# K in one transfer per block, its last quarter copied aside on ScalarE, and wo read two heads at a time, in a cached decode attention kernel

## The chip, the cores and the metric

The kernel runs on one core of a Trainium2 chip. The metric is the device time of one execution in microseconds (us). The core has TensorE (PE: matmuls, and PEld, the weight loads), VectorE (DVE), ScalarE (ACT), GpSimd (POOL) and SyncE (SP), which here does nothing but issue transfers; 16 DMA engines move data between HBM and the on-chip memory SBUF.

## The reference, cut to what matters

One token of decode attention, mixed by a gate with a small token mixer. With D = 448, 16 query heads, 8 key/value heads (so two query heads share one), 65,536 cached keys and head size 256, all in bf16:

```python
g = sigmoid((x * gate_w).sum(-1, keepdims=True))
q = (x @ wq)                                   # 16 heads of 256
scores = einsum("bhqd,bhkd->bhqk", q, repeat(k_cache, 2)) * 256 ** -0.5
o = einsum("bhqk,bhkd->bhqd", softmax(scores), repeat(v_cache, 2))
a = o.reshape(1, 1, 4096) @ wo                 # 4096 x 448
b = gelu_mlp_over_tokens(layernorm(x))         # w1, b1, w2, b2
return g * a + (1 - g) * b
```

The K and V caches are 8 x 65,536 x 256 bf16 each, 268 MB each, and every byte is read once.

## The kernel before, in words

The caches are cut into 32 blocks of 16,384 keys (`NBLK`, four blocks per key/value head, `NB = 4`); block n has K(n) and V(n) of 8 MB each. `L` is the last block, 31. A block lies in SBUF as 128 partitions by 128 keys by 256 (64 KB in each partition). K lies in two tiles `kn0` and `kn1` of 64 keys per partition each (32 KB rows), V in one tile `vt`. There is one buffer for K and one for V: each is filled again when its readers are done, piece by piece, for the dependencies go by the bytes that are touched.

For each block, `score_block` (L370) goes through eight slices of 16 keys per partition. For each slice, `transposes` (L354) is one VectorE instruction that turns the slice into one of two buffers `kT`, and `scores` (L362) is eight matmuls into one PSUM tile. `softmax` (L416) then finds the maximum, takes the exponential on ScalarE (L441) and transposes the result into `pT` (L449). `products` (L510) multiplies with V in 64 matmuls (L384) and adds into an accumulator. At the end of every fourth block `head_end` (L497) normalises the result and multiplies it by two heads of `wo` (L493).

A helper `seq` keeps each engine's instructions in program order, so the order on the queues is the order of the Python code. In the main loop (L529 to L580), for block n up to 29, SyncE issues V(n) (L121; it waits until the products of block n-1 have read `vt`), then the two halves of K(n+1) (L115; the first waits for transposes 0 to 3 of block n, the second for 4 to 7). The transfers run in one queue behind each other. In block 0, `load_wo` (L129) then reads the first 14 heads of `wo` into the tile `wo_sb`, whose first part has served until then as the buffer `gel` of the mixer (written at L255, read at L321).

The end has an order of its own. In block 30 the queue gets the first 48 keys per partition of V(30) (3 MB), the two halves of K(31), and the rest of V(30) (5 MB). In block 31 V(31) is read in eight pieces into the buffers of K (L136), each as soon as the transposes of block 31 have left its place, and then the last two heads of `wo`. At the start, K(0) is read in three pieces, and `vt` holds the weights `wq` until the queries are made.

Of the kernel before, what the change touches and what calls it, by code (L numbers as in the profile page):

```python
# [8 lines left out]
FP32 = mybir.dt.float32  # L9
BF16 = mybir.dt.bfloat16  # L10
# [4 lines left out]
HQ = 16  # L15
HKV = 8
DH = 256
REP = HQ // HKV

BLK = 16384  # L20
VP = BLK // 128
KP = VP // 2
NJ = 16
NI = VP // NJ
NQ = 4
NW = DH // 2 // 32
QW = 128 + 2 * NI


@with_exitstack  # L30
def kernel(
# [15 lines left out]
    nc = tc.nc  # L47

    D = A_x.shape[-1]
# [3 lines left out]
    NF = F // 128  # L53
    NB = SK // BLK
    NBLK = HKV * NB
# [4 lines left out]
    def seq(ins):  # L60
        e = ins.ins.engine
        if e in last:
            tc.add_manual_dep(
                ins.ins,
                last[e],
                mybir.DependencyInfo(
                    mybir.DependencyClass.NoSync, mybir.DependencyReason.DATA
                ),
                reason="program order",
            )  # L70
        last[e] = ins.ins.name
        return ins

    kvpool = ctx.enter_context(tc.tile_pool(name="kvpool", bufs=1))
    const = ctx.enter_context(tc.tile_pool(name="const", bufs=1))
# [2 lines left out]


    kvpool.tile([128, 4096 - 128], mybir.dt.uint8, name="fill")  # L80
    k_tiles = [kvpool.tile([128, KP, DH], BF16, name=f"kn{i}") for i in range(2)]
    vt = kvpool.tile([128, VP, DH], BF16, name="vt")
    kT_tiles = [kvpool.tile([128, NJ, NW, 32, 2], BF16, name=f"kT{i}") for i in range(2)]
    p_sb = work.tile([128, 512], BF16)
    pT_tiles = [work.tile([128, 512], BF16, name=f"pT{i}") for i in range(2)]
    wo_sb = const.tile([128, HQ, 2, D], BF16)

    sc_tiles = [psum.tile([128, 512], FP32, name=f"sc{i}") for i in range(2)]
    pv_ps = psum.tile([128, 2, DH], FP32, name="pv_ps")
# [1 line left out]
    MC = D // 2  # L91
# [12 lines left out]
    DM = 384  # L104
    wq_m = vt[:, 0:48, :].rearrange("p a b -> p (a b)").rearrange("p (k n) -> p k n", k=3)
    wq_t = vt[:, 48:56, :].rearrange("p a b -> p (a b)")
    gel = wo_sb[:].rearrange("p h c n -> p (h c) n")[:, 0:NF, :]

    def rows(cache, n):
        g, b = divmod(n, NB)  # L110
        return cache[0, g, b * BLK:(b + 1) * BLK, :].rearrange("(p j) d -> p j d", j=VP)

    def load_k(n, h, pieces=((0, KP),)):
        for j0, j1 in pieces:
            seq(nc.sync.dma_start(  # L115
                out=k_tiles[h][:, j0:j1, :],
                in_=rows(A_k_cache, n)[:, h * KP + j0:h * KP + j1, :],
            ))

    def load_v(n, j0=0, j1=VP):  # L120
        seq(nc.sync.dma_start(out=vt[:, j0:j1, :], in_=rows(A_v_cache, n)[:, j0:j1, :]))  # L121

# [4 lines left out]

    def load_wo(h0, h1):
        seq(nc.sync.dma_start(  # L129
            out=wo_sb[:, h0:h1],  # L130
            in_=A_wo[h0 * DH:h1 * DH, :].rearrange("(h p c) n -> p h c n", p=128, c=2),
        ))

    def load_v_last(n):
# [9 lines left out]
        out=wq_t[:, :], in_=A_wq[DM:D, :].rearrange("r (h n) -> (r h) n", h=2)  # L144
    ))
    with nc.allow_non_contiguous_dma(reason="short rows"):
# [16 lines left out]
        out=val[:], in_=rowsel[:, :, :, 0:NI], op=ALU.add, axis=AXIS.XY  # L163
    ))
    fst = const.tile([128, 2, REP], FP32)
    for e in range(2):
        seq(nc.vector.tensor_reduce(
            out=fst[:, e, :], in_=rowsel[:, :, :, e:e + 1], op=ALU.add, axis=AXIS.XY
# [3 lines left out]
        out=par[:], in_=ident_f[:].rearrange("p (a r) -> p r a", r=REP), op=ALU.add, axis=AXIS.X  # L172
# [3 lines left out]
        out=nval[:], in0=val[:], scalar1=-scale, scalar2=None, op0=ALU.mult  # L176
# [7 lines left out]
        out=same[:], in_=val[:].unsqueeze(1).to_broadcast([128, 64, REP])  # L184
# [4 lines left out]
    for i in range(2):  # L189
# [3 lines left out]
        out=sel[:],  # L193
        in_=ident[:].rearrange("p (w k) -> p w k", w=NW).unsqueeze(2).to_broadcast([128, NW, NQ, 32]),
# [7 lines left out]
        out=xrr[:], in_=xr[:, DM:D].unsqueeze(2).to_broadcast([1, D - DM, 2])  # L202
    ))
    x_col = hd_ps[:, 40:44]
    for k in range(3):
        seq(nc.tensor.matmul(
            x_col[:, k:k + 1], lhsT=xr[:, 0:DM].rearrange("o (p k) -> o k p", k=3)[:, k, :],
            rhs=ones_b[:, 0:1], start=True, stop=True,
# [3 lines left out]
        rhs=ones_b[:, 0:1], start=True, stop=True,  # L212
# [6 lines left out]
        out=xtm[:], in0=par[:], scalar1=x_col[:, 3:4], scalar2=None, op0=ALU.mult  # L219
# [17 lines left out]
        out=veps[:], in0=mv[:, 1:2], scalar1=1e-5, scalar2=None, op0=ALU.add  # L237
# [5 lines left out]
    for _ in range(2):  # L243
# [3 lines left out]
            out=ntmp[:], in0=ntmp[:], scalar1=-0.5, scalar2=1.5, op0=ALU.mult, op1=ALU.add  # L247
# [3 lines left out]
        out=h_bc[:], in0=xf[:], scalar1=mv[:, 0:1], scalar2=rstd[:, 0:1],  # L251
        op0=ALU.subtract, op1=ALU.mult,
    ))
    for b in range(NF):
        seq(nc.scalar.activation(  # L255
            out=gel[:, b, :], in_=h_bc[:], func=ACT.Gelu_apprx_tanh,
# [4 lines left out]
    for h in range(HQ):  # L261
        half, hh = divmod(h, HQ // 2)
        for c in range(2):
            col = c * HQ + h
            for k in range(3):
                seq(nc.tensor.matmul(
                    q_ps[:, col:col + 1],
                    lhsT=wq_m[:, k, h * DH:(h + 1) * DH].rearrange("p (d c) -> p c d", c=2)[:, c, :],
                    rhs=xm[:, k:k + 1],
# [5 lines left out]
                lhsT=wq_t[:, hh * DH:(hh + 1) * DH].rearrange("p (d c) -> p c d", c=2)[:, c, :],  # L275
                rhs=xtm[:, half:half + 1],
# [6 lines left out]
    for w in range(NW):  # L283
        seq(nc.tensor.matmul(
            qq_ps[:, w * 2 * HQ:(w + 1) * 2 * HQ],
            lhsT=sel[:, w, :, :].rearrange("p a k -> p (a k)"), rhs=qb[:],
# [60 lines left out]
    oT = work.tile([128, 2, REP], BF16)  # L347
# [2 lines left out]
    res = const.tile([1, D], BF16)  # L350
    gcol = const.tile([128, 1], FP32)

    def transposes(i):
        seq(nc.vector.transpose(  # L354
            out=kT_tiles[i % 2][:].rearrange("p j w k c -> p (j w k c)").bitcast(FP32),
            in_=k_tiles[i // 4][:, i % 4 * NJ:(i % 4 + 1) * NJ, :].rearrange("p j d -> p (j d)").bitcast(FP32),
        ))

    def scores(n, i):
        for w in range(NW):  # L360
# [7 lines left out]
                ))  # L368

    def score_block(n, hooks={}):  # L370
        for i in range(NI):
            transposes(i)
            scores(n, i)
            if i in hooks:
                hooks[i]()
        if n % NB == 1 and n < NBLK - NB:
            place_q(n // NB + 1)
# [110 lines left out]
    def project(g):  # L488
        a_ps = hd_ps[0:1, 0:D]
        for r in range(REP):  # L490
            for c in range(2):
                seq(nc.tensor.matmul(  # L492
                    a_ps, lhsT=oT[:, c, r:r + 1], rhs=wo_sb[:, g * REP + r, c, :],  # L493
                    start=(r == 0 and c == 0), stop=(r == REP - 1 and c == 1),
                ))

    def head_end(g):  # L497
# [6 lines left out]
            seq(nc.vector.tensor_copy(out=a_acc[:], in_=a_ps))  # L504
        else:
            seq(nc.vector.tensor_tensor(out=a_acc[:], in0=a_acc[:], in1=a_ps, op=ALU.add))  # L506

    L = NBLK - 1

    def products(n):  # L510
        for ip in range(NI // 2):
# [17 lines left out]
    for n in range(NBLK):  # L529
        if n == 0:  # L530
            score_block(n, {2: gate_sum, 5: mixer_tail})
        elif n < L:
            score_block(n, {1: gate_column} if n == 1 else {})
        else:
            score_block(n, {1: result_base, 2: lambda: pv(L - 1, 0), 3: lambda: pv_one(L - 1, 2)})
        if n < L - 1:
            load_v(n)
            load_k(n + 1, 0)
            load_k(n + 1, 1)
            if n == 0:  # L540
                load_wo(0, HQ - REP)
        elif n == L - 1:
            load_v(n, 0, 48)
            load_k(L, 0)
            load_k(L, 1)
            load_v(n, 48, VP)
        else:
            load_v_last(L)
            for h in range(HQ - REP, HQ):
                load_wo(h, h + 1)  # L550
        if n < L:
            softmax(n)
        else:
            def rest_base():
                for k in range(2):
                    seq(nc.tensor.matmul(
                        f_rows[k], lhsT=ident_f[0:1, 0:1], rhs=base[0:1, k * MC:(k + 1) * MC],
                        start=True, stop=False, tile_position=(0, 32 * k),
                    ))
                pv(L - 1, 2, range(4, NJ))  # L560

            softmax(n, [lambda: pv_one(L - 1, 3), lambda: pv(L - 1, 2, range(4)), rest_base])
            seq(nc.vector.tensor_scalar(
                out=lsv[:], in0=val[:], scalar1=lsum[:, 0:1], scalar2=None, op0=ALU.mult
            ))
            pv(L - 1, 3)
            accumulate(L - 1)
            seq(nc.tensor.matmul(
                sm_ps[:, 456:456 + REP], lhsT=ones_f[:, :], rhs=lsv[:, :], start=True, stop=True
            ))  # L570
            seq(nc.vector.reciprocal(out=rdv[:], in_=sm_ps[:, 456:456 + REP]))
            seq(nc.vector.tensor_scalar(
                out=rdv[:], in0=rdv[:], scalar1=gcol[:, 0:1], scalar2=None, op0=ALU.mult
            ))
        if n < L - 1:
            if n % NB == NB - 1:
                denominators()
            products(n)
            if n % NB == NB - 1:
                head_end(n // NB)  # L580
# [6 lines left out]
    for c in range(2):  # L587
        for e in range(2):
# [3 lines left out]
                rhs=fst[:, e, :],  # L592
# [6 lines left out]
    for r in range(REP):  # L599
        for c in range(2):  # L600
            for k in range(2):
                seq(nc.tensor.matmul(  # L602
                    f_rows[k], lhsT=oT[:, c, r:r + 1],
                    rhs=wo_sb[:, HQ - REP + r, c, k * MC:(k + 1) * MC],
                    start=False, stop=(r == REP - 1 and c == 1),
                    tile_position=(0, 32 * k),
                ))
# [33 lines left out]
```

## Time and profile before

| what | value |
|---|---|
| median of 3 runs | 1272.16 us (1271.48 to 1272.31) |
| span of the profiled execution, first to last instruction | 1270.1 us |
| busy: TensorE matmul / weight load | 785.6 us (62%) / 306.3 us (24%) |
| busy: VectorE / ScalarE | 683.8 us (54%) / 43.1 us (3%) |
| read from HBM | 544.22 MB, 428 GB/s over the span |
| packets in SyncE's queue | 17,506, for 99.4% of the time of 16 DMA engines |
| mean granted TensorE clock | 0.81 |

The profiled execution has no other time than its span; the timed runs are other executions, and their median is 2.0 us above that span. The profile gives for every instruction its engine, its line in the kernel, its start and duration, and what it waited for. "SPq" is SyncE's issue of a transfer; "DMA vt<-in_A_v_cache_dram" in a chain is the time between an issue and the landing. Every packet of the 16 DMA engines is also on record with its start, duration and size; a packet of one of these transfers is one row of one partition.

### The profile page before, as it was taken

The page shows a single profiled execution, that of the slowest core. Times are in us where ns is not written, and L with a number is a line of the kernel's source. Part 1 is how long each engine was busy: PE and PEld are TensorE (multiplying, and loading weights), DVE is VectorE, ACT ScalarE, POOL GpSimd, SP SyncE. Part 2 cuts the span into 40 slices and gives each one's busy share as a digit, 9 for nine tenths or more (in the row PEclk, how much of TensorE's full clock was granted, in tenths as well). Part 3 has the DMA queues.
Part 4 walks back from the last instruction along what each step waited for, and adds up shares of the span by engine and source line. Part 5 has one row for each costly group of instructions (what it writes and reads, how often), then busy time and mean ns, then how long its engine had stood idle before and what let it go on. Part 6 is the DMA issues. An engine that isn't in the chain of part 4 may idle for free.

```text
span 1270.1 us, 10381 instructions
## 1 busy us (share of the span) xinstructions
PE 785.6 (62%) x4577; PEld 306.3 (24%) x4577; DVE 683.8 (54%) x619; ACT 43.1 (3%) x108; POOL 2.7 (0%) x8
## 2 busy tenths in 40 slices
PE   4656566565556666575765566655657556676566
PEld 2222222222222222122222222212222222222223
DVE  5465455665446654456554466645566444665473
ACT  4000000000000000000000000000000000000000
POOL 0000000000000000000000000000000000000000
PEclk9787778887788877878777878877887778887787
DMA  9999999999999999999999999999999999999998
GB/s 412 423 435 431 432 426 431 434 443 432 428 432 434 435 432 434 431 430 431 441 430 431 430 438 438 435 428 430 433 432 441 438 429 425 433 439 432 423 413 336
DMA packets 17989, 544.90 MB, mean 429 GB/s; under 512 B 2197, under 2 KB 4248, under 8 KB 4760
## 3 DMA queue, kind: packets, MB, share of 16 engines
q1 hardware_dynamic: 17506, 544.22, 99.4%
q8 instruction: 36, 0.59, 0.2%
q10 hardware_dynamic: 438, 0.01, 0.0%
q14 instruction: 9, 0.07, 0.0%
HBM read 544.22 MB, written 0.00 MB: 428 GB/s over the span
## 4 chain that ended last, share of the span: by engine, by line
DMA 80%; PE 15%; DVE 4%; issue 2%; ACT 0%; ACTq 0%; SPq 0%; DVEq 0%
DMA vt<-in_A_v_cache_dram 62%; DMA kn<-in_A_k_cache_dram 15%; PE pv_ps L384 11%; PE sc L362 3%; DVE kT L354 3%; DMA kn<-in_A_v_cache_dram 2%; DMA w1b<-in_B_w_dram 1%; PE hd_ps L321 0%; PE hd_ps L492 0%; PE f L602 0%; ACT p_sb L441 0%; DVE acc L459 0%; DVE pT L449 0%; DVE rmax L422 0%; DVE y_sb L325 0%
## 5 line engine op out<-in xcount | busy, mean ns | idle before, releaser
L362 PE MATMUL sc<-kT,qz 128*128 128x512 bf16 x2048 | 550.7, 419 | 246.6 <-DVE kT L354 246.4
L354 DVE STREAM_TRANSPOSE kT<-kn 128x2048 f32<-128x2048 f32 x256 | 571.2, 2282 | 128.1 <-DMA kn<-in_A_k_cache_dram 79.7
L362 PEld LDWEIGHTS <-qz 128*128 128x128 bf16 x2048 | 210.7, 104 | 586.0 <-issue 227.9
L384 PE MATMUL pv_ps<-vt,pT 128*4 128x512 bf16 x1968 | 176.0, 535 | 158.1 <-DMA vt<-in_A_v_cache_dram 156.3
L459 DVE SCALAR_TENSOR_TENSOR acc<-acc,al,pv_ps 128x512 f32<-128x512 f32 x23 | 17.2, 747 | 213.3 <-PE pv_ps L384 213.3
L384 PEld LDWEIGHTS <-pT 128*4 128x4 bf16 x2000 | 59.6, 110 | 267.1 <-issue 207.3
L441 ACT ACTIVATE p_sb<-sc,nb 128x512 bf16<-128x512 f32 x32 | 22.0, 687 | 1193.0 <-DVE nb L437 1193.0
L422 DVE TENSOR_REDUCE rmax<-sc 128x1 f32<-128x512 f32 x32 | 22.1, 691 | 60.4 <-PE sc L362 60.4
L464 DVE COPY acc<-pv_ps 128x512 f32<-128x512 f32 x8 | 5.5, 691 | 72.5 <-PE pv_ps L384 72.5
L449 DVE STREAM_TRANSPOSE pT<-p_sb 128x512 bf16<-128x512 bf16 x32 | 22.8, 711 | 28.9 <-ACT p_sb L441 28.9
L424 PE MATMUL sm_ps<-ident_f,rmax 128*1 128x128 f32 x32 | 8.7, 270 | 24.5 <-DVE rmax L422 24.5
L433 PE MATMUL sm_ps<-mrun,ones_f 1*128 1x2 f32 x64 | 12.1, 256 | 13.8 <-DVE mrun L432 11.4
L433 PEld LDWEIGHTS sm_ps<-mrun,ones_f 1*128 1x128 f32 x64 | 9.4, 182 | 20.0 <-DVE mrun L432 16.1
L437 DVE CUSTOM_DVE_ANT_0 junk<-sm_ps,nval 128x2 f32<-128x2 f32 x32 | 5.1, 159 | 15.1 <-PE sm_ps L433 15.1
L424 PEld LDWEIGHTS sm_ps<-ident_f,rmax 128*1 128x1 f32 x32 | 2.5, 79 | 40.2 <-DVE rmax L422 40.2
L467 PE MATMUL hd_ps<-lsum,same 128*128 128x1 f32 x14 | 3.5, 319 | 13.8 <-DVE lsum L451 13.8
L426 DVE TENSOR_REDUCE mnew<-sm_ps 1x2 f32<-1x64 f32 x24 | 5.1, 212 | 8.7 <-PE sm_ps L424 8.7
L255 ACT ACTIVATE wo_sb<-h_bc,b1f,w1f 128x448 bf16<-128x448 f32 x14 | 9.2, 747 | 6.7 <-DVE h_bc L250 6.7
L492 PE MATMUL hd_ps<-wo_sb,oT 128*1 128x448 bf16 x28 | 8.4, 395 | 0.0
L481 PE MATMUL hd_ps<-esc,acc 128*128 128x2 f32 x28 | 4.4, 263 | 6.0 <-DVE acc L459 6.0
L446 ACT ACTIVATE al<-nb,nb 128x1 f32<-128x1 f32 x24 | 6.8, 283 | 0.0
L506 DVE TENSOR_TENSOR a_acc<-a_acc,hd_ps 1x448 f32<-1x448 f32 x6 | 3.7, 608 | 5.5 <-PE hd_ps L492 5.5
(103 smaller groups left out, 108.2 us busy)
## 6 DMA issues: line engine op xcount, KB each, us to landing
kn<-in_A_k_cache_dram SPq DMA_DIRECT2D x63, 4096.0 KB, 28.5
vt<-in_A_v_cache_dram SPq DMA_DIRECT2D x1, 5120.0 KB, 29.9
kn<-in_A_k_cache_dram SPq DMA_DIRECT2D x2, 2048.0 KB, 12.3
kn<-in_A_v_cache_dram SPq DMA_DIRECT2D x2, 2048.0 KB, 21.2
wo_sb<-in_A_wo_dram SPq DMA_DIRECT2D x1, 3136.0 KB
vt<-in_A_wq_dram SPq DMA_DIRECT2D x1, 3072.0 KB, 10.1
vt<-in_A_v_cache_dram SPq DMA_DIRECT2D x1, 3072.0 KB
kn<-in_A_v_cache_dram SPq DMA_DIRECT2D x3, 1024.0 KB
```

The costliest lines, as they stand in the source:

```text
L255: seq(nc.scalar.activation(out=gel[:, b, :], in_=h_bc[:], func=ACT.Gelu_apprx_tanh, scale=w1f[:, b:b + 1], bias=b1f[:, b:b + 1],))
L354: seq(nc.vector.transpose(out=kT_tiles[i % 2][:].rearrange("p j w k c -> p (j w k c)").bitcast(FP32), in_=k_tiles[i // 4][:, i % 4 * NJ:(i ...
L362: seq(nc.tensor.matmul(sc_tiles[n % 2][:, :], lhsT=qz_tiles[n // NB % 2][:, 2 * w + c, 2 * (NI - i):2 * (NI - i) + 128], rhs=kT_tiles[i % ...
L384: seq(nc.tensor.matmul(dst[32 * grp:32 * grp + 2 * REP, :, :], lhsT=pT[:, 32 * jj + 2 * REP * ip:32 * jj + 2 * REP * (ip + 1)], rhs=pairs( ...
L422: seq(nc.vector.tensor_reduce(out=rmax[:], in_=sc_ps[:, :], op=ALU.max, axis=AXIS.X))
L424: seq(nc.tensor.transpose(sm_ps[0:1, 0:128], rmax[:, 0:1], ident_f[:, :]))
L433: seq(nc.tensor.matmul(sm_ps[:, 128:128 + REP], lhsT=ones_f[0:1, :], rhs=mrun[0:1, :], start=True, stop=True))
L441: seq(nc.scalar.activation(out=p_sb[:, :], in_=sc_ps[:, :], func=ACT.Exp, scale=scale, bias=nb[:, 0:1], accum_out=den[:, 0:1],))
L446: seq(nc.scalar.activation(out=al[:], in_=nb_old[:], func=ACT.Exp, scale=-1.0, bias=nb[:, 0:1]))
L449: seq(nc.vector.transpose(out=pT[:, :], in_=p_sb[:, :]))
L459: seq(nc.vector.scalar_tensor_tensor(out=acc[:], in0=acc[:], scalar=al_tiles[n % 2][:, 0:1], in1=src[:, :, :], op0=ALU.mult, op1=ALU.add,))
L492: seq(nc.tensor.matmul(a_ps, lhsT=oT[:, c, r:r + 1], rhs=wo_sb[:, g * REP + r, c, :], start=(r == 0 and c == 0), stop=(r == REP - 1 and c ...
```

## The change

- The two K tiles become one tile `kn` of 128 keys per partition. K(2) to K(30) come in one transfer of 64 KB rows (`load_k_whole`). K(0), K(1) and K(31) still come in pieces.
- In blocks 1 to 30, ScalarE copies the last two slices of K (`NS = 2`, a quarter of the block) into a tile `spare` at the block's start (`set_aside`), and transposes 6 and 7 read from there. The other six slices are read from `kn`.
- `wo` is held two heads at a time in two tiles; two heads are read after every first block of a head group (n = 1, 5, ... 25). The last two heads are read at the end as before.
- `gel` moves from `wo_sb` to `spare`.

```diff
+NS = 2
-    k_tiles = [kvpool.tile([128, KP, DH], BF16, name=f"kn{i}") for i in range(2)]
+    kn = kvpool.tile([128, VP, DH], BF16, name="kn")
+    k_tiles = [kn[:, i * KP:(i + 1) * KP, :] for i in range(2)]
     vt = kvpool.tile([128, VP, DH], BF16, name="vt")
+    spare = kvpool.tile([128, NS * NJ, DH], BF16, name="spare")
-    wo_sb = const.tile([128, HQ, 2, D], BF16)
+    wo_tiles = [const.tile([128, REP, 2, D], BF16, name=f"wo{i}") for i in range(2)]
...
-    gel = wo_sb[:].rearrange("p h c n -> p (h c) n")[:, 0:NF, :]
+    gel = spare[:].rearrange("p j d -> p (j d)")[:, 0:NF * D].rearrange("p (b n) -> p b n", n=D)
...
+    def load_k_whole(n):
+        seq(nc.sync.dma_start(out=kn[:, :, :], in_=rows(A_k_cache, n)))
...
     def load_wo(h0, h1):
         seq(nc.sync.dma_start(
-            out=wo_sb[:, h0:h1],
+            out=wo_tiles[h0 // REP % 2][:, h0 % REP:(h1 - 1) % REP + 1],
...
-    def transposes(i):
+    def transposes(src, i):
         seq(nc.vector.transpose(
             out=kT_tiles[i % 2][:].rearrange("p j w k c -> p (j w k c)").bitcast(FP32),
-            in_=k_tiles[i // 4][:, i % 4 * NJ:(i % 4 + 1) * NJ, :].rearrange("p j d -> p (j d)").bitcast(FP32),
+            in_=src.rearrange("p j d -> p (j d)").bitcast(FP32),
         ))
+
+    def key_slice(n, i):
+        if 0 < n < L and i >= NI - NS:
+            i0 = i - (NI - NS)
+            return spare[:, i0 * NJ:(i0 + 1) * NJ, :]
+        return kn[:, i * NJ:(i + 1) * NJ, :]
+
+    def set_aside(n):
+        for i in range(NI - NS, NI):
+            seq(nc.scalar.copy(out=key_slice(n, i), in_=kn[:, i * NJ:(i + 1) * NJ, :]))
...
     def score_block(n, hooks={}):
+        if 0 < n < L:
+            set_aside(n)
         for i in range(NI):
-            transposes(i)
+            transposes(key_slice(n, i), i)
             scores(n, i)
...
         if n < L - 1:
             load_v(n)
-            load_k(n + 1, 0)
-            load_k(n + 1, 1)
             if n == 0:
-                load_wo(0, HQ - REP)
+                load_k(1, 0)
+                load_k(1, 1)
+            else:
+                load_k_whole(n + 1)
+            if n % NB == 1 and n < NBLK - NB:
+                load_wo(n // NB * REP, (n // NB + 1) * REP)
         elif n == L - 1:
             load_v(n, 0, 48)
             load_k(L, 0)
```

More of the change, by code (lines that the diff above doesn't have):

```diff
@@ L351 @@
     gcol = const.tile([128, 1], FP32)
-    def transposes(i):
+    L = NBLK - 1
+    def transposes(src, i):
         seq(nc.vector.transpose(
             out=kT_tiles[i % 2][:].rearrange("p j w k c -> p (j w k c)").bitcast(FP32),
-            in_=k_tiles[i // 4][:, i % 4 * NJ:(i % 4 + 1) * NJ, :].rearrange("p j d -> p (j d)").bitcast(FP32),
+            in_=src.rearrange("p j d -> p (j d)").bitcast(FP32),
         ))
+    def key_slice(n, i):
[6 more added lines that the diff above has]
+            seq(nc.scalar.copy(out=key_slice(n, i), in_=kn[:, i * NJ:(i + 1) * NJ, :]))
     def scores(n, i):
@@ L492, in project @@
                 seq(nc.tensor.matmul(
-                    a_ps, lhsT=oT[:, c, r:r + 1], rhs=wo_sb[:, g * REP + r, c, :],
+                    a_ps, lhsT=oT[:, c, r:r + 1], rhs=wo_tiles[g % 2][:, r, c, :],
                     start=(r == 0 and c == 0), stop=(r == REP - 1 and c == 1),
@@ L506, in head_end @@
             seq(nc.vector.tensor_tensor(out=a_acc[:], in0=a_acc[:], in1=a_ps, op=ALU.add))
-    L = NBLK - 1
     def products(n):
@@ L603 @@
                     f_rows[k], lhsT=oT[:, c, r:r + 1],
-                    rhs=wo_sb[:, HQ - REP + r, c, k * MC:(k + 1) * MC],
+                    rhs=wo_tiles[(HKV - 1) % 2][:, r, c, k * MC:(k + 1) * MC],
                     start=False, stop=(r == REP - 1 and c == 1),
```

## The prediction

> **What bounds the kernel now.** I read the slices of the page first, then the table of queues, the chain of waits, and last the timelines of the places that the change touches.
>
> ```profile
> DMA  9999999999999999999999999999999999999998
> GB/s 412 423 435 431 432 426 431 434 443 432 428 432 434 435 432 434 431 430 431 441 430 431 430 438 438 435 428 430 433 432 441 438 429 425 433 439 432 423 413 336
> q1 hardware_dynamic: 17506, 544.22, 99.4%
> q8 instruction: 36, 0.59, 0.2%
> ```
>
> The DMA engines are busy from end to end (99.4% by SyncE's queue alone), TensorE 62%, VectorE 54%. So only two things can move the time: what a byte costs in a busy queue, and stretches in which the queue is empty. One block (K(n) and V(n), 8 MB each) takes about 38.7 us of DMA.
>
> The order of compute in one steady block (timeline, block 3):
>
> ```profile
> 147.04 4.50 DVE L354 STREAM_TRANSPOSE kT<-kn 128x2048 f32<-128x2048 f32 x2 [3.87 <-DMA kn<-in_A_k_cache_dram]
> 153.04 13.28 DVE L354 STREAM_TRANSPOSE kT<-kn 128x2048 f32<-128x2048 f32 x6 [1.50 <-PE sc L362]
> 171.30 0.71 DVE L449 STREAM_TRANSPOSE pT<-p_sb 128x512 bf16<-128x512 bf16 x1 [0.90 <-ACT p_sb L441]
> 176.14 6.05 PE L384 MATMUL pv_ps<-vt,pT 128*4 128x512 bf16 x64 [3.38 <-DMA vt<-in_A_v_cache_dram]
> ```
>
> The eight transposes start when the first half of K lands, 9.7 us before the second half. Transposes 0 to 3 end about 10.5 us after the start, 0 to 5 about 15.0 us (14.5 to 15.8 over blocks 2 to 30), pT 25 us.
>
> The last two blocks are different, because V(30) is split around K(31). SyncE's queue and VectorE there:
>
> ```profile
> 1189.68 0.33 SPq L121 DMA_DIRECT2D vt<-in_A_v_cache_dram  x1
> 1206.22 10.05 SPq L115 DMA_DIRECT2D kn<-in_A_k_cache_dram  x2
> 1216.32 0.42 SPq L121 DMA_DIRECT2D vt<-in_A_v_cache_dram  x1
> 1195.69 4.50 DVE L354 STREAM_TRANSPOSE kT<-kn 128x2048 f32<-128x2048 f32 x2 [2.57 <-DMA kn<-in_A_k_cache_dram]
> 1201.69 4.50 DVE L354 STREAM_TRANSPOSE kT<-kn 128x2048 f32<-128x2048 f32 x2 [1.50 <-PE sc L362]
> 1207.03 8.89 DVE L354 STREAM_TRANSPOSE kT<-kn 128x2048 f32<-128x2048 f32 x4 [0.83 <-DMA kn<-in_A_k_cache_dram]
> ```
>
> The DMA rate in two stretches there (the last three columns are granted clock, DMA share and GB/s):
>
> ```profile
> 1205.00:1210.00 5.00, 3.47 (x16) 1.37 (x15) 4.17 (x3) 0.00 (x0) 0.00 (x0) 1.00 0.94 374
> 1217.00:1222.00 5.00, 1.52 (x8) 0.56 (x5) 2.03 (x7) 0.96 (x3) 0.00 (x0) 1.00 0.89 301
> ```
>
> K(31,0) is issued at 1206.22, as transpose 3 of block 30 ends. Even today that is just too late for some DMA engines: the rate falls to 374 GB/s. The packet records say which: the 16 engines are not level. Instructions are fetched in 16 KB packets, one a block, and each costs one engine 1.42 us (0.93 its own, 0.5 in the next packet); it hits about half of the engines. By block 30 the slowest is 7.5 us behind the fastest. The fast ones went idle at 1206.3; the slowest, which sets every landing, did not.
>
> **The change part by part.** The sum is made against the profiled execution: span 1270.1 us; the median of the runs, 1272.16, is 2.0 above it, and I put the sum's change on that median.
>
> *64 KB rows.* K(2) to K(30), 29 blocks. In the packet records one engine finishes the two halves of a K block 9.681 us apart each, 19.362 together, and a V block, which has 64 KB rows, in 19.319. Each whole K saves 0.043 us: 29 x 0.043 = **-1.25 us**. It is on the path, as the queue is.
>
> *The copies.* Two of 128x4096 bf16 a block for blocks 1 to 30, 60 in all. No such row is there. Lower bound by slope: the 128x512 exponential takes 687 ns, the 128x1 one 283, so 0.79 ns an element and 3.5 us a copy; upper bound in proportion, 8 x 687 = 5.5 us. I take 3.5, since long rows spread the fixed part. They start with transpose 0 and end 7 to 11 us after it, before transpose 5 ends at 15.0, so they are hidden by transposes 0 to 5: price zero. Behind them on ScalarE is only the exponential of the block, at 23 us. Transposes 6 and 7 read the spare buffer from 15 us on. If ScalarE slowed VectorE's reads, transpose 5 would be late, which the next step prices.
>
> *Transposes wait for all of K.* They move 9.7 us later against the transfers. pT is then ready 25.3 us after K(n) has landed, by when V(n) (19.3 us) is there; products of 5 to 6.5 us end at 31 to 33 and release V(n+1), which is needed at 38.7. The stall of the products on V (3.38 us above) goes, and nothing is late: zero.
>
> *K(n+1) is issued after transpose 5 and the copies.* That is 0.35 (landing to first transpose, block 30: 1195.36 to 1195.69) + 15.0 = 15.4 us after K(n) landed, up to 16.2. The slowest engine runs dry at 19.3, so the issue leads by 3.1 to 4 us. What lead is enough? K(31,1), issued 1215.94, reached engines that ran dry 1.6 and 2.1 us later with a gap, first packets up to 3.3 us after the issue; an engine that ran dry 5.1 us after the issue of K(31,0) had no gap. So the price lies between 0 and about 2 us a block. I take 0, since 3.3 is the longest way seen and most leads exceed it. The fast engines will wait, which costs nothing while they stay ahead of the slowest. Queued behind K(n+1) on SyncE are only wo and V(n+1), not due until 31 us.
>
> *wo.* 14 heads in one transfer of about 8 us behind K(1) become seven of 1.2 us behind K(2), K(6), ... K(26): same 1792-byte rows, six more transfers at a 9 ns semaphore packet each; zero. V(1) loses that cover: issued at 62.51 with K(1) landing at 71.1, it leads by 7 us on the fast engines, still enough. The wait of wo on gel's readers goes to the copies of block 1 (K(1) lands at 71, the readers ended at 45): zero.
>
> *The last whole K.* Block 30 still takes K(30) whole, but V(30) is only 3 MB ahead of K(31,0), 7.3 us. K(31,0) overwrites the tiles of transposes 0 to 3, which now start only at the full landing: 0.35 + 10.5 + 0.05 = 10.9 us after it. All engines are dry for 3.6 us, and then restart. A restart: at the program's start, issue at 0.74, the last of 16 engines finished its eight 0.912 us packets at 10.51, so 10.51 - 0.74 - 7.3 = 2.47; the idle engines at 1206.22 needed 1.66. I take 2.47, as all 16 start and the slowest counts. K(31,0) lands 10.9 + 2.47 + 9.7 = 23.1 us after K(30). Before, those two landings were 1206.5 and 1224.1, 17.6 apart (7.3 + 9.7 + 0.6 of slow packets). Loss **+5.5 us**; ends 4.2 (transposes 10.2, restart 1.66, slow packets again) to 8 (transposes 11.3, restart 3.9 as engines at 1215.94 had it). Behind it, K(31,1), the rest of V(30), V(31) and wo follow back to back as today, so nothing is regained.
>
> *After the restart the engines are level*, so an instruction fetch in the last 50 us (one at 1242.6) hits an engine that has no reserve: 0 to +1.4, I take **+0.5**.
>
> Sum: -1.25 + 5.5 + 0.5 = **+4.75 us**: span 1274.9, median 1276.9, +0.37%. A measurement of this kernel tells about 0.2% (2.5 us) from no change.
>
> **The rivals.**
> *A, the issue of K(n+1) is too late in every block.* For: the gaps with leads up to 2.1 us and first packets 3.3 us after issue, against leads of 3.1 to 4; idle engines restart with first packets of 1.9 to 2.4 us in place of 1.21, and an instruction fetch (1.42) can push one of those past the slowest. Against: the 5.1 us case, and 0.98 us from issue to packet at 1206.22. Between 0.2 and 2 us x 29, so 6 to 58 more; at 0.7 it gives 1276.9 + 20 = 1297.
> *B, the end costs less.* With TensorE warm from the first slice, four transposes take 4 x 2.2 = 8.8 us; with a 1.66 restart K(31,0) lands 20.5 after K(30), loss 2.9; no fetch: +1.7, 1273.8, no difference to be told. Against: in each of blocks 2 to 30 the third transpose waits for slow matmuls.
> *C, faster: fewer transfer starts.* If each transfer's start (2.47 us at the program's start) were paid in the queue, 29 fewer would give 72 us, 1205; it decides once a start costs over 0.25 us in the queue. Against: the halves follow each other at 9.681 us, their bytes alone; chance 0.03. The Trainium skill's page "DMA: Bandwidth & Descriptors" (section "Anatomy of one DMA") gives a fixed cost of about 2.0 us for each DMA on the GpSimd path; taken for these transfers it would make 58 us of gain by 29 of them, and the same spacing of 9.681 us speaks against it here.
> *D, faster: instruction fetches stop hurting.* If they fell on engines that wait for K(n+1) instead of on the slowest, its 7.5 us would go: 1276.9 - 7.5 = 1269.4. For: such idle time will exist in each block. Against: the slowest has none. Chance 0.05.
>
> **How the numbers follow.** Forecast 0.62, with its own range 1274.8 to 1281; A 0.18; B 0.12; C and D 0.08 together. Faster 0.08, same 0.12, slower 0.80. The range for 8 in 10 takes half of B and the lower part of A: 1273.5 to 1292.
>
> **What would show it.** Right: K transfers of 64 KB packets, SyncE's K issue 15 to 16 us after K lands, DMA share still 0.99 to 1.00 between 100 and 1150 us; block period 38.8 us; products no longer waiting on V; copies near 3.5 us; a hole of 5 to 6 us in the DMA rate about 1212 to 1218, with K(31,0) issued as transpose 3 of block 30 ends, some 10 us after that block's first. Wrong: a dip of the rate in every block, or transposes well over 2.2 us beside the copies (A); a span under 1270 (C, D).

## The result, and the profile after

The changed kernel takes 1288.7 us (median of 4 runs, 1285.4 to 1293.8) against 1272.08 us before (1271.5 to 1272.3): a ratio of 1.0136, 95% interval 1.0117 to 1.0155, 16.6 us slower. The sign and the stated range were right, the forecast of 1276.9 was 11.8 us short, and its own range, 1274.8 to 1281, missed. The runs also lie further apart, over 8 us where they lay within 1. The profiled execution is the slowest of the four (span 1291.8 us), so amounts are taken below from the medians of runs, and the profile shows the mechanism.

The slices and the queue of the changed kernel, from its page:

```profile
DMA  9999999999999999999999999999999999999988
GB/s 407 427 443 434 431 425 431 427 427 442 427 412 412 427 433 427 410 423 432 427 439 413 419 436 417 429 417 407 445 431 428 429 427 425 423 429 441 398 343 356
q1 hardware_dynamic: 13426, 544.22, 98.6%
```

The packets fall from 17,506 to 13,426: the 64 KB rows are there. The digits of busy time look as before, but the rates are lower in many slices. A stretch that leaves out both ends shows it better (the last three columns are clock, DMA share, GB/s). Before:

```profile
100.00:1150.00 1050.00, 655.91 (x3655) 251.48 (x3651) 566.92 (x484) 24.65 (x74) 0.00 (x0) 0.80 1.00 433
```

After:

```profile
100.00:1150.00 1050.00, 621.51 (x3518) 239.41 (x3519) 552.87 (x472) 215.87 (x126) 0.00 (x0) 0.80 1.00 426
```

The DMA engines count as busy 1.00 of the time in both, and move 433 and 426 GB/s. A busy share tells how long packets were under way, not how fast they went: for the most part the packets themselves became slower (what idle time the rounded 1.00 hides stands in a table further down).

The groups of the changed kernel's page that answer to the prediction's steps:

```profile
L375 ACT COPY spare<-kn 128x4096 bf16<-128x4096 bf16 x60 | 213.4, 3603 | 463.6 <-DMA kn<-in_A_k_cache_dram 463.6
L404 PE MATMUL pv_ps<-vt,pT 128*4 128x512 bf16 x1968 | 157.7, 491 | 45.5 <-DVE pT L469 26.3
```

The products' row before:

```profile
L384 PE MATMUL pv_ps<-vt,pT 128*4 128x512 bf16 x1968 | 176.0, 535 | 158.1 <-DMA vt<-in_A_v_cache_dram 156.3
```

A copy takes 3.60 us (3.5 was taken). The products hardly wait for V any more; 45.5 us of idle time are left before them where there were 158.1, and most of it is ended by VectorE's pT. Both steps came out as worked out.

One K issue in the middle, by the chain of waits (start, duration, what):

```profile
785.72 2.32 DVE kT L362
788.04 0.05 issue
788.08 6.48 PE sc L380 x16
794.57 0.02 issue
794.59 0.04 DVE kT L362
...
799.02 2.28 DVE kT L362
801.30 0.02 SPq L124
801.32 0.03 issue
801.35 25.56 DMA kn<-in_A_k_cache_dram
```

and the stretches around it:

```profile
801.00:803.00 2.00, 1.71 (x9) 0.77 (x8) 2.00 (x2) 0.00 (x0) 0.00 (x0) 1.00 1.12 393
803.00:805.00 2.00, 1.71 (x9) 0.67 (x7) 2.00 (x2) 0.00 (x0) 0.00 (x0) 1.00 0.52 197
```

Transpose 5 ends 15.6 us after transpose 0 started, since the third and fourth had to wait for slow matmuls (6.48 us for 16), and SyncE issues K at once. It lands 25.56 us later. In the stretches a row counts where it begins, so a single rate is coarse; the packet records are exact. V(19) landed on the engines between 801.65 and 804.56. 13 of the 16 engines were through with V within 1.83 us of the issue and stood idle before their first row of K. Nine of these rows begin 0.96 to 1.26 us after the issue and take 0.45 to 1.26 us longer than the usual 2.418; the other four begin only 2.3 to 3.8 us after it. The next rows of the nine are stretched too, by 0.2 to 0.4 us, and so are rows of the three engines that never were idle: the first row of the slowest, which begins at 804.56, and the second rows of the other two (806.02 and 806.17) take 0.35 to 0.36 longer. V to K took 19.3 us from landing to landing on an undisturbed engine; K(20) lands 2.6 us later than that.

The end of the changed kernel: SyncE's queue, then VectorE, then the stretches.

```profile
1210.82 0.33 SPq L127 DMA_DIRECT2D vt<-in_A_v_cache_dram  x1
1232.38 4.76 SPq L118 DMA_DIRECT2D kn<-in_A_k_cache_dram  x2
1237.19 0.43 SPq L127 DMA_DIRECT2D vt<-in_A_v_cache_dram  x1
```

```profile
1222.14 4.50 DVE L362 STREAM_TRANSPOSE kT<-kn 128x2048 f32<-128x2048 f32 x2 [8.84 <-DMA kn<-in_A_k_cache_dram]
1227.85 8.89 DVE L362 STREAM_TRANSPOSE kT<-kn 128x2048 f32<-128x2048 f32 x4 [1.20 <-PE sc L380]
```

```profile
1222.00:1226.00 4.00, 1.49 (x4) 0.56 (x5) 3.86 (x2) 3.80 (x2) 0.00 (x0) 0.50 1.00 430
1226.00:1230.00 4.00, 3.55 (x13) 1.30 (x12) 2.80 (x2) 3.31 (x1) 0.00 (x0) 0.83 0.19 78
1230.00:1234.00 4.00, 3.50 (x16) 1.51 (x16) 4.00 (x3) 0.00 (x0) 0.00 (x0) 1.00 0.52 115
```

The hole that was forecast is there: K(31,0) is issued at 1232.38, as transpose 3 of block 30 ends, 10.2 us after that block's first transpose, and the rate falls to 78 and 115 GB/s. K(31,0) lands 22.9 us after K(30) (23.1 was forecast, 17.6 before).

So the end accounts for some 5 to 6 us. The rest, about 11 us in the medians, is lost in the blocks. The landings of the two profiled executions show it as well: in the changed kernel K(30) lands 15.3 us later than before, and from there to the last packet it takes 6.4 us longer. Two theories for it, and a third to be kept out:

- *Late issue*: K(n+1) reaches DMA engines that are dry. What costs is the lead, the time from the issue until they run dry.
- *Fetch*: the engines are held level, so each instruction fetch (1.42 us on one engine) hits one without reserve.
- *Copy*: the copies disturb the transfers, or wo in pieces does.

### The profile page after: what moved, and what is told of

It reads as the page before. It is cut to its first block, busy times and chain, and to the rows that moved or that the text cites. A ratio compares the mean times of both kernels' runs of the same rounds, so it can differ in the third digit from the quotient of the medians.

```text
span 1291.8 us, 10427 instructions
## 1 busy us (share of the span) xinstructions
PE 766.2 (59%) x4577; PEld 300.3 (23%) x4577; DVE 684.2 (53%) x619; ACT 256.4 (20%) x168; POOL 2.7 (0%) x8
## 3 DMA queue, kind: packets, MB, share of 16 engines
q1 hardware_dynamic: 13426, 544.22, 98.6%
## 4 chain that ended last, share of the span: by engine, by line
DMA 64%; issue 12%; PE 12%; DVE 12%; ACT 1%; SPq 0%; ACTq 0%; DVEq 0%
DMA kn<-in_A_k_cache_dram 59%; DVE kT L362 11%; PE sc L380 11%; DMA vt<-in_A_v_cache_dram 2%; DMA kn<-in_A_v_cache_dram 2%; DMA w1b<-in_B_w_dram 1%; ACT spare L375 1%; PE hd_ps L327 0%; PE f L623 0%; DVE y_sb L331 0%; SPq L124 0%; DVE rest L337 0%; ACTq L147 0%; DVE rest L334 0%; PE hd_ps L429 0%
## 5 line engine op out<-in xcount | busy, mean ns | idle before, releaser
L362 DVE STREAM_TRANSPOSE kT<-kn 128x2048 f32<-128x2048 f32 x196 | 439.7, 2287 | 282.4 <-DMA kn<-in_A_k_cache_dram 232.4
L375 ACT COPY spare<-kn 128x4096 bf16<-128x4096 bf16 x60 | 213.4, 3603 | 463.6 <-DMA kn<-in_A_k_cache_dram 463.6
L404 PE MATMUL pv_ps<-vt,pT 128*4 128x512 bf16 x1968 | 157.7, 491 | 45.5 <-DVE pT L469 26.3
L362 DVE STREAM_TRANSPOSE kT<-spare 128x2048 f32<-128x2048 f32 x60 | 133.9, 2271 | 0.2 <-DVE kT L362 0.2
L404 PEld LDWEIGHTS <-pT 128*4 128x4 bf16 x2000 | 53.8, 103 | 140.6 <-issue 70.6
L453 PEld LDWEIGHTS sm_ps<-mrun,ones_f 1*128 1x128 f32 x64 | 9.4, 183 | 20.0 <-DVE mrun L452 16.1
L457 DVE CUSTOM_DVE_ANT_0 junk<-sm_ps,nval 128x2 f32<-128x2 f32 x32 | 5.1, 160 | 15.1 <-PE sm_ps L453 15.1
L261 ACT ACTIVATE spare<-h_bc,b1f,w1f 128x448 bf16<-128x448 f32 x14 | 9.2, 746 | 6.7 <-DVE h_bc L256 6.7
L512 PE MATMUL hd_ps<-wo,oT 128*1 128x448 bf16 x28 | 8.0, 375 | 0.0
## 6 DMA issues: line engine op xcount, KB each, us to landing
vt<-in_A_v_cache_dram SPq DMA_DIRECT2D x1, 5120.0 KB, 30.6
```

The lines of the kernel that those rows point to most:

```text
L261: seq(nc.scalar.activation(out=gel[:, b, :], in_=h_bc[:], func=ACT.Gelu_apprx_tanh, scale=w1f[:, b:b + 1], bias=b1f[:, b:b + 1],))
L362: seq(nc.vector.transpose(out=kT_tiles[i % 2][:].rearrange("p j w k c -> p (j w k c)").bitcast(FP32), in_=src.rearrange("p j d -> p (j d)" ...
L375: seq(nc.scalar.copy(out=key_slice(n, i), in_=kn[:, i * NJ:(i + 1) * NJ, :]))
L404: seq(nc.tensor.matmul(dst[32 * grp:32 * grp + 2 * REP, :, :], lhsT=pT[:, 32 * jj + 2 * REP * ip:32 * jj + 2 * REP * (ip + 1)], rhs=pairs( ...
L453: seq(nc.tensor.matmul(sm_ps[:, 128:128 + REP], lhsT=ones_f[0:1, :], rhs=mrun[0:1, :], start=True, stop=True))
L512: seq(nc.tensor.matmul(a_ps, lhsT=oT[:, c, r:r + 1], rhs=wo_tiles[g % 2][:, r, c, :], start=(r == 0 and c == 0), stop=(r == REP - 1 and c ...
```

## The experiments

**Three slices set aside in place of two.** A 1792-byte buffer that two steps share makes the room.

```diff
-NS = 2
+NS = 3
...
-    base = const.tile([1, D], FP32)
+    base = zt
```

> Three slices of K are set aside instead of two, so K(n+1) is released by transpose 4 (about 13.4 us after K(n) landed, before 15.4) and by three copies of 3.6 us (11.2 us). Late-issue theory (K(n+1) reaches DMA engines that are dry, and their restart stretches packets): the lead on the slowest engine grows from about 4 to 6 us and most of the loss per block goes, only the loss at the end stays: 1276 to 1280 us. Fetch theory (the engines are held level, so that each instruction fetch of 1.42 us hits an engine without reserve): the fast engines may run 2 us further ahead, about half of the loss per block goes: 1281 to 1285. Copy theory (ScalarE's copies disturb the transfers): half as many copies again, 1291 or more. One 1792-byte buffer is shared by two uses to make room; nothing else differs.

1276.74 us (ratio 1.0037, 1.0025 to 1.005). With half as many copies again, 12 of the 16.6 us are gone. The same long stretch as above, of this kernel:

```profile
100.00:1150.00 1050.00, 645.00 (x3571) 247.17 (x3571) 565.63 (x480) 310.58 (x153) 0.00 (x0) 0.79 1.00 433
```

433 GB/s, as before the change. K(30) lands 2.0 us earlier than in the profile before, and from there to the last packet it takes 6.2 us longer. The copy theory falls. The fetch theory expected 1281 to 1285 and missed: the fetches are as many as ever.

**The end undone alone.**

```diff
-        if 0 < n < L and i >= NI - NS:
+        if 0 < n < L - 1 and i >= NI - NS:
...
-        if 0 < n < L:
+        if 0 < n < L - 1:
             set_aside(n)
...
-            if n == 0:
-                load_k(1, 0)
-                load_k(1, 1)
+            if n == 0 or n == L - 2:
+                load_k(n + 1, 0)
+                load_k(n + 1, 1)
```

> As the changed kernel, but K(30) comes in its two halves and block 30 reads all slices in place, so K(31,0) can be issued about 1 us after K(30) has landed. If the hole before K(31,0) costs what the two traces say (landing to landing 22.9 us against 17.6, and 1.1 us for a fetch behind it): 5 to 6.5 us less than the changed kernel, 1282 to 1284. If the end has slack that the hole only uses up: no difference, 1288.

1281.0 us (1.0061, 1.0038 to 1.0083; runs from 1275.5 to 1282.2), 7.7 us less than the changed kernel and 1 to 3 us below what was expected. The end has no slack. As the loss in the blocks varies from run to run, this is no clean measure of the end; the pair of runs with three slices, below, is.

**K in two halves, with everything else of the change.**

```diff
-                load_k_whole(n + 1)
+                load_k(n + 1, 0)
+                load_k(n + 1, 1)
```

> As the changed kernel with its copies and its wo, but every K comes in its two halves of 32 KB rows; the first is released by transpose 3, the second by transpose 5 and the copies. Late-issue theory: nothing is dry any more, 1272 to 1273, as the kernel before. Copy theory, or wo in pieces being the cost: 1282 or more.

1271.66 us, ratio 0.9997 (0.9988 to 1.0007): no difference from before. Copies, spare buffer, the move of gel and wo in pieces cost nothing together. All of the loss hangs on the one transfer.

**No copies, whole K released by the last transpose.**

```diff
-        if 0 < n < L and i >= NI - NS:
+        if n < 0:
...
-        if 0 < n < L:
+        if n < 0:
             set_aside(n)
```

> As the changed kernel with whole K, but without any copy: all eight transposes read K in place, so K(n+1) is issued only after transpose 7, some 19.7 us after K(n) landed, when V(n) (19.3 us) is through. Late-issue theory: every engine runs dry in every block, 19.7 + 2.2 (restart) + 19.3 = 41.2 us a block in place of 38.7 and of about 39.4 in the changed kernel: 1340 to 1355. Copy theory: the copies are gone, so no more than the changed kernel, 1289 or less.

1350.9 us (1.0618, 1.0602 to 1.0634), as late issue has it. Its long stretch:

```profile
100.00:1150.00 1050.00, 592.56 (x3359) 227.94 (x3359) 524.54 (x448) 22.91 (x69) 0.00 (x0) 0.78 0.95 405
```

Here the engines are idle in earnest: share 0.95.

**Three slices, and the end undone.** Both edits above together.

> Three slices set aside, and K(30) in halves with block 30 reading in place: no late issue in the blocks and no hole before K(31,0). What is left of the change is 28 K blocks in 64 KB rows at 0.043 us each, 1.2 us less than the kernel before: 1270.5 to 1271.3. If the smaller descriptors' price was not real, or the levelled engines still lose to fetches: 1272 or more.

1270.27 us, ratio 0.9988 (0.998 to 0.9997): 1.5 us faster than the kernel before, where 1.2 was worked out from 28 blocks at 0.043. It is the only kernel here that beats it, and by less than 0.2%. Against the run with three slices alone, each by its own runs of before (+4.7 and -1.5), the end costs 6.2 us.

**The release put off by a constant.** With three slices, ScalarE copies the last slice once more, so that its copies release K(n+1), at the same time after the landing in every block.

```diff
     def set_aside(n):
         for i in range(NI - NS, NI):
             seq(nc.scalar.copy(out=key_slice(n, i), in_=kn[:, i * NJ:(i + 1) * NJ, :]))
+        seq(nc.scalar.copy(out=key_slice(n, NI - 1), in_=kn[:, (NI - 1) * NJ:NI * NJ, :]))
```

> Three slices set aside, and the last one is copied a second time, so that ScalarE (four copies of 3.6 us) and not VectorE releases K(n+1), 14.8 us after K(n) landed in every block: the slowest engine has 4.6 us of lead (6.2 with three copies, about 4 in the changed kernel). Graded theory (an engine needs about 2 us of lead; the slowest one's lead less 2 us is all the spread that the engines may have, and instruction fetches of 1.42 us use it up): part of the loss comes back, 1278 to 1284. Jitter theory (only blocks with late transposes lose): none comes back, 1277 as with three copies.

1277.44 us (1.0046, 1.0032 to 1.006). Nothing came back. The graded theory was wrong at this point: a lead of 5 us on the slowest engine is enough.

With another half copy:

```diff
+        seq(nc.scalar.copy(out=key_slice(n, NI - 1)[:, 0:NJ // 2, :], in_=kn[:, (NI - 1) * NJ:(NI - 1) * NJ + NJ // 2, :]))
```

> As the run with the release at 14.8 us, with another half copy of 1.9 us: release 16.7 us after K(n) landed, 2.7 us of lead on the slowest engine, later than in the changed kernel. Graded theory: nearly every engine is dry or close to it at each issue, 1292 to 1306. If the loss in the changed kernel came from something other than the time of release (VectorE's reads of the spare buffer, the copies as such): 1289 or less.

1308.1 us (1.0286, 1.0272 to 1.03), 2 us above the range of the graded theory and worse than the changed kernel, with one slice fewer to wait for on VectorE and the same K transfers. 1.9 us of delay cost 30.6 us, 1.05 a block.

With a quarter copy in place of the half (`NJ // 4`):

> As the run with the release at 14.8 us, with another quarter copy of about 1.1 us, so that K(n+1) is released by ScalarE at about 15.8 us after K(n) landed in every block (15.4 by the last packet of K), 3.8 us of lead on the slowest engine: close to the changed kernel's mean, but with no spread from VectorE's transposes. If the mean lead decides: between the runs at 14.8 (1277) and 16.7 (1308), near the changed kernel, 1285 to 1292. If in the changed kernel only its latest blocks pay (a threshold above 15.8 us): 1277 to 1280.

1293.65 us (1.0175, 1.0158 to 1.0192), 1.7 above the range for the mean lead and far from the other theory's 1277 to 1280. The chain of waits there names the copies as what releases K:

```profile
785.69 10.63 ACT spare L375 x3
796.32 0.02 issue
796.34 3.61 ACT spare L376
799.95 0.02 issue
799.98 1.05 ACT spare L377
```

**A small first piece.** Is it the release after the landing that counts, or what is still queued? The run was made to answer this; the release was meant to stay as it is.

```diff
     def load_k_whole(n):
-        seq(nc.sync.dma_start(out=kn[:, :, :], in_=rows(A_k_cache, n)))
+        for j0, j1 in ((0, NJ), (NJ, VP)):
+            seq(nc.sync.dma_start(out=kn[:, j0:j1, :], in_=rows(A_k_cache, n)[:, j0:j1, :]))
```

> The changed kernel with its two copies, but each whole K comes as a first piece of one slice (8 KB rows, released by transpose 0, 2.4 us of transfer) and the other seven slices (56 KB rows, released by transpose 5 and the copies as before). Late-issue theory: the release of the large part stays at about 15.4 us, but 2.4 us more are queued ahead of it, so the lead is 6.4 us and the loss per block goes; block 30 starts one transpose earlier, so the hole at the end is some 1 to 2.5 us smaller: 1273.5 to 1277. If the time of release after the landing is what costs, and not what is queued: 1287 to 1290.

1276.83 us (1.0038, 1.0025 to 1.0052). The loss in the blocks is gone. But the release did not stay unchanged. VectorE, ScalarE and SyncE after a landing:

```profile
697.75 4.50 DVE L363 STREAM_TRANSPOSE kT<-kn 128x2048 f32<-128x2048 f32 x2 [8.00 <-DMA kn<-in_A_k_cache_dram]
697.73 7.11 ACT L376 COPY spare<-kn 128x4096 bf16<-128x4096 bf16 x2 [17.05 <-DMA kn<-in_A_k_cache_dram]
710.94 0.33 SPq L125 DMA_DIRECT2D kn<-in_A_k_cache_dram  x1
```

Transpose 0 reads the small piece and is done before the large part lands, so only transposes 1 to 5 are left, and the next large part is issued 13.3 us after the landing (mean of the 22 blocks of the table below), where the changed kernel takes 15.6. With 1 MB more queued ahead of it as well, release and lead both became better, and this run does not tell them apart. The end of the changed kernel does: K(31,0) is issued 10.6 us after the last packet of K(30), earlier than any release in the table, and yet every engine is dry by then, for the 3 MB of V(30) ahead of it were through 3.3 us before. It is the lead that counts.

The kernels side by side. Release and lead are means over the 22 blocks with no wo behind K, from the packet records of one execution each: from the last packet of K(n) to the issue of K(n+1), and from that issue until V is through on the slowest and on the fastest engine. Dry and stretched time are sums per DMA engine over blocks 2 to 28; the kernel before has 0.3 and 1.1 us (the latter is its fetches).

| kernel | release, us | lead, slowest / fastest | dry / stretched, us | time, us |
|---|---|---|---|---|
| three slices | 13.4 | 6.4 / 3.3 | 0.1 / 2.2 | 1276.7 |
| one copy more | 14.7 | 5.1 / 2.5 | 0.6 / 2.7 | 1277.4 |
| the change | 15.6 (15.0 to 16.1) | 4.2 / 1.5 | 6.4 / 13.0 | 1288.7 |
| 1 1/4 copies more | 15.7 | 4.2 / 1.6 | 5.0 / 12.3 | 1293.7 |
| 1 1/2 copies more | 16.6 | 3.3 / 0.8 | 14.5 / 19.3 | 1308.1 |
| no copies | 19.8 | 0.5 / -1.2 | 55.6 / 19.9 | 1350.9 |

The step lies between 14.7 and 15.6 us, where the mean lead falls from 5.1 to 4.2 us on the slowest engine and from 2.5 to 1.5 on the fastest. The blocks of the changed kernel say it again. With 2 us or more on the fastest engine (6 blocks) K landed late by 0, 0, 0, 0, 0.05 and 0.8 us, with less (16 blocks) by 0.8 us on average and by up to 2.6. Sorted by the slowest engine's lead they part still further: with 4.2 us or more (10 blocks) K was 0.15 us late on average, with less (12 blocks) 1.0. And a short lead on the fastest engine alone costs little: in the run with one copy more, 7 of the 22 blocks have less than 2 us there and at least 4.5 on the slowest, and K was 0.13 us late in them on average, against 0.11 over all 22. As far as these blocks show, it is by the slowest engine's lead that K was late or not. And just behind the step the loss is less idle time than stretched packets, 6.4 against 13.0 us in the changed kernel.

## Why the prediction was right or wrong

*64 KB rows, -1.25 us.* Right: the kernel that keeps them and loses nothing gains 1.5 us.

*The copies, zero.* Right: 3.60 us each, done some 7.5 us after the landing, and the run with halves has them all and is no slower.

*Transposes wait for all of K, zero; wo, zero.* Right: for the transposes by the products' waits and by the run with three slices and the end undone, where they wait for all of K too; for `wo` by the run with halves.

*K(n+1) is issued after transpose 5 and the copies, zero.* This is the step that failed, and it is nearly the whole difference between forecast and result. The time of the issue was right (15.4 us forecast, 15.6 in the mean), and the bounds held: 0 to 2 us a block, and about 12 us over 29 blocks are 0.4. Wrong was the end that I took, with both its reasons. The first was that 3.3 us is the longest way seen and most leads exceed it: in the changed kernel 20 of the 22 leads of the slowest engine exceed 3.3 us, and in 8 of these 20 blocks K is late by more than 0.5 us. The second was "The fast engines will wait, which costs nothing while they stay ahead of the slowest". When engines that ran dry restart, their first rows take up to 1.3 us longer, and rows of the others become longer in the same microseconds, the slowest's too. So the slowest engine's lead has to cover the restart of the others as well; about 4.2 us were enough here. The profile before had shown it: engines with 1.6 and 2.1 us of lead had gaps after the issue at 1215.94, and between 1219 and 1222 rows of all others were stretched, by 0.5 to 0.9 us and less. The prediction entered that as "0.6 of slow packets" in another term, and did not see in it what would happen in every block. Its rival A had the place right and 20 us for its middle; the result lies between the forecast and A. That the stated range holds the result is owed to A, whose lower part it took in, and not to the forecast's own mechanism. Why a restart stretches the rows of other engines, the records do not say; that stays open.

The spread of the runs fits the same step: in the changed kernel the release hangs on transposes that wait for matmuls at a changing granted clock (0.50 to 1.00 in the stretches above), and its 15.0 to 16.1 us lie on the step. Where ScalarE sets the release at 14.7 or 15.7 us, four runs each lie within 1.5 us.

*The last whole K, +5.5, and a fetch behind it, +0.5.* Right: 22.9 us between the landings against 17.6 is 5.3, and from there to the last packet it took 43.7 us where it had taken 42.5; a fetch at 1264.4 sets one engine back in that time, and the engines are level by then (they finish K(31,0) within 0.5 us of each other). That second part was 1.15 us and not 0.5. Together 6.4 by the traces, 6.2 by the runs with three slices, 6.0 forecast.

*B* (a cheap end) fell with this. *C* (a start paid for each transfer) fell: 28 fewer starts bring 1.5 us, not 72. *D* (fetches that stop hurting) did not come: with three slices and the end undone the gain is that of the rows.

The sum with the measured sizes: -1.5 for the rows, +6.2 for the end, and +11.9 for the late issue (16.6 less the 4.7 that three slices leave) make 16.6. These are differences along one chain of kernels, so they add up by themselves; what supports the split are the landings, which give 15.3 us up to K(30) and 6.4 behind it in the one execution that was profiled (21.7 us longer than the profile before), and the run with halves.

## What to carry to other kernels

When a queue of transfers is meant to be full, compare GB/s in the same stretch and not the busy share alone: late issues show as slow packets before they show as idle engines. Look at each DMA engine: the landing of the transfer ahead is the last one's, the first ran dry about 3 us before it, and the restart of the early ones stretches the rows of the last. Here nothing much was lost while an issue led the last engine by some 4.2 us or more; a release could slip by 1.4 us without harm, and the next microsecond cost 0.56 us a block (1277.4 to 1293.7 over 29). A transfer that is made larger to save its overhead waits for the last reader of all its bytes: the saving was 0.043 us a block, and the release came 5.2 us later after the landing than that of the second half had (15.1 against 9.9 in block 3).

## What the runs showed of the hardware that I had not expected

While some DMA engines restart, the others are slower too: in the changed kernel 561 of 9451 packets between the last packets of K(2) and K(29) took more than 30 ns longer than their size's usual time, 36 of 11,678 before. A dry engine's first packet begins there 0.96 us after the issue at the earliest, and in the issue at 801.35 the nine rows that began first took 2.9 to 3.7 us in place of 2.418. The Trainium skill's page "DMA: Bandwidth & Descriptors" (section "Anatomy of one DMA") puts about 2 us of fixed cost on each DMA of the GpSimd path, most of it at the completion, after the last byte. For these transfers, which SyncE issues, a cost of that size is seen at the start, and only where an engine has run dry: at that issue 0.96 to 1.26 us before the first row and 0.45 to 1.26 within it. Back to back, 28 fewer transfers brought 1.5 us together.

Instruction fetches are not free to a kernel that is bound by transfers: all but two of the 36 fetches of 16 KB in the kernel before take 0.88 to 0.96 us of one DMA engine, and they lengthen its next packet by about 0.5. The Trainium skill's page "Runtime: NRT & Kernel Launch" (section "Instruction fetch mechanics") calls the crossing of a 16 KiB boundary mostly hidden. By block 30, after 33 fetches, the slowest DMA engine was 7.5 us behind the fastest, where it had been 1.9 in block 2.
